# Attention block of a transformer layer: token rows of x permuted over the partitions, and V loaded in three two-row pieces a tile

## Chip, cores and metric

The kernel runs on one core of one Trainium2 chip. The metric is the device time of one execution in microseconds (us), as the median of three runs. An engine name stands for its instruction queue: PE is the matrix engine (TensorE), DVE the vector engine, ACT the scalar engine, POOL GpSimd, and SP the engine that issues nearly all transfers (DMAs).

## The reference, cut to what matters

One transformer layer on 2048 tokens of width 512, in bf16. `mod` gives six vectors from a condition `c`: shift, scale and gate for each of two halves.

```
h = layernorm(x) * (1 + ca) + sa
q, k, v = split(h @ wqkv)                # 32 heads of width 16
logits[s, w] = q[s] . k[s - 2*w] / 4     # w = 0..7; before the first token: -1e9
o[s] = sum over w of softmax(logits)[s, w] * v[s - 2*w]
x = x + ga * (o @ wo)
h = layernorm(x) * (1 + cb) + sb
x = x + gb * ((silu(h @ w1) * (h @ w3)) @ w2)    # inner width 1792
```

Each token looks at itself and at seven earlier tokens, two apart.

## The kernel before, in words

The tokens are cut into 16 tiles T of 128. Token number 128*T + p lies on partition p. A small planner's result is written into the file: `ORDER` is a list of operation numbers, and every engine works through its own operations in the order in which they stand in that list, waiting on semaphores for what they need. `SLOTS` says which buffer each value gets. So an operation that waits holds up everything behind it on its engine, SP's DMA issues among them. A DMA is issued by `Program.dma` (L117, the issue itself is L127).

Stages of the work, with the names that matter below:

- **Loads.** x comes in six DMAs: tiles 0 and 1 alone, 2 and 3 together, then three times four tiles (`x_view`, "(t p) d -> p t d": 128 rows of 1 KB a tile, partition outermost). The modulation weights `wm_s[0]` come in four DMAs (two for the scale, two for the shift, 256 KB each), `wqkv` in six of 256 KB (two each for q, k and v), `wo` in four. The tiny load of `c` (4 rows of 256 bytes) and one of 32 rows of 256 bytes are issued by ACT.
- **First layernorm.** DVE takes statistics of each tile (L579, L580), POOL the power -0.5 (L584, L586), DVE or ACT normalizes. PE turns tiles 0 to 11 with an identity as the moving operand (L663), ACT and DVE evict with the modulation (L672, L673, L680). Tiles 12 to 15 are turned by DMA transposes, and ACT applies the modulation in place (L648).
- **Projections.** k and q (L722, with `wqkv` as the stationary operand; 256 columns a matmul for the first two groups of two tiles, 512 for the others) and v (L749). V is stored to DRAM behind 16 rows of zeros (`v_dram`). Fifteen matmuls on ones (L542) fill the wait for the first data.
- **Attention, by tile.** DVE multiplies q with the eight shifted k's (`prod`, L780, 4096 elements a partition). PE sums over each head's 16 channels with a matrix of ones and zeros `E_sb` (L791, four column groups of 32). Softmax runs on pairs of tiles (L803, L808, ACT's exp L821, L833, L835, L836), and DVE's 32x32 transpose L840 puts the weights beside the V rows. V is loaded again from DRAM, 1 MB a tile in four DMAs of 256 KB: each partition holds two tokens at one of the eight offsets. DVE multiplies in place (`av`, L862, 4096 elements), PE sums over the offsets (L871), ACT evicts (L877), a DMA transposes (`sb_ot`), PE multiplies with `wo` (L895), DVE adds to x (L899).
- **Second layernorm and FFN**, by groups of 2, 2, 4, 4 and 4 tiles: statistics on ACT (L614), POOL (L620, L621), transposes on PE for the first two groups and by DMA for the others, then L911 (w1 and w3), L917, L921, L922, L925, and L953 and L941 with w2. DVE adds x (L969), and one DMA a tile stores 128 rows of 1 KB. Tiles 14 and 15 are stored in two column pieces each.

SP's issues begin with x0, x1, x2-3, the two scale pieces, the two k pieces, the two shift pieces, the two v pieces, x4-7, one q piece, x8-11, the other q piece, x12-15.

Of the kernel before, what the change touches and what calls it, by code (L numbers as in the profile page):

```python
# [21 lines left out]
PAD = 16  # L22
EPS = 1e-5
# [47 lines left out]
def packet_ns(size):  # L71
    return {256: 18, 512: 27, 768: 36, 1024: 48, 2048: 92}[size]


class Program:
# [41 lines left out]
    def dma(self, out, in_, key, packets, r=(), w=(), part=(), after=(), eng="sp", cost=450, group=None, transpose=False,  # L117
            store=False, again=False, pre=()):
        nc = self.nc

        def fn(e):
            a = out() if callable(out) else out
            b = in_() if callable(in_) else in_
            with nc.allow_non_contiguous_dma(reason="layout"):
                for pa, pb in pre:
                    e.dma_start(pa, pb).then_inc(o.inc[0], 16)
                return e.dma_start(a, b, transpose=True) if transpose else e.dma_start(a, b)  # L127
# [3 lines left out]
        ns = 600 if transpose else each * ((PACKET if pre == () and not SHIFTED else 84) if again else packet_ns(size)) + 170 * len(pre)  # L131
        o = self.op(eng, fn, cost, key, r=r, w=w, part=part, after=after, dma=(each, ns, *((900, 200) if store else (1300, 600))))
        o.count = 1 + len(pre)
# [13 lines left out]
    def place(self, order, slots):  # L147
# [10 lines left out]
        for at, o in enumerate(self.placed):  # L158
# [3 lines left out]
            for v in o.vals:  # L162
                if v.pool is not None and v.pool.last.get(v.slot) is not v:
                    before = v.pool.last.get(v.slot)
                    if before is not None:
                        o.prev.extend(before.users)
                    v.pool.last[v.slot] = v

    def synchronize(self):
        known = {e: {} for e in ENGINES}  # L170
        waited = set()
        for o in self.placed:
            e = o.eng
            need = {}
            for d, true in list(o.deps.items()) + [(d, False) for d in o.prev]:
# [77 lines left out]
C_PQ, C_RED, C_ACC, C_TINY = 2203, 440, 864, 90  # L253
# [17 lines left out]
PACKET = 122  # L271
SHIFTED = False
NWARM = 15
DMA_T = (4, 2)
AVCOL = frozenset(range(16))
# [5 lines left out]
def _build(p, A_x, A_wqkv, A_wo, B_w1, B_w3, B_w2, c, w_mod, out):  # L281
# [4 lines left out]
    x_view = x2d.rearrange("(t p) d -> p t d", p=P)  # L286
# [10 lines left out]
    kT = sb([P, KT, PAD + S], bf, "kT")  # L297
# [4 lines left out]
    vshb = [sb([P, 8, D], bf, f"vsh{i}") for i in range(2)]  # L302
# [11 lines left out]
    E_sb = sb([P, KT, H], bf, "E")  # L314
    ones = sb([P, 512], bf, "ones")
    ind = sb([P, 2, 16, 2], bf, "ind")
    before = sb([P, 2, W, 4, 8], bf, "before")
# [26 lines left out]
    zrow = at([PAD, D], bf, "zrow", 25600)  # L344
# [8 lines left out]
    skew = nc.dram_tensor("skew_dram", (NT, 16, 4160), bf) if SHIFTED else None  # L353
# [11 lines left out]
    vshpool = pqpool = Pool("big", pqb + vshb)  # L365
# [8 lines left out]
    def held(pool, items):  # L374

        vals = []
        for i, item in enumerate(items):
# [5 lines left out]
    big_hold = held(vshpool, [vsh_x, vsh_q])  # L383
# [3 lines left out]
    vc, vident, vcst, vE, vind, vbefore = (Val(n) for n in ("const", "ident", "cst", "E", "ind", "before"))  # L387
# [11 lines left out]
    p.op("pool", lambda e: e.memset(E_sb[:], 1.0), 150, k, w=[vE])  # L399
    p.op("pool", lambda e: e.affine_select(out=E_sb[:], in_=E_sb[:], compare_op=ALU.is_ge, fill=0.0, base=0,  # L400
                                           pattern=[[128, KT], [-16, H]], channel_multiplier=1), 320, k, w=[vE])
    p.op("pool", lambda e: e.affine_select(out=E_sb[:], in_=E_sb[:], compare_op=ALU.is_ge, fill=0.0, base=15,
                                           pattern=[[-128, KT], [16, H]], channel_multiplier=-1), 320, k, w=[vE])
    p.op("pool", lambda e: e.memset(ind[:], 0.0), 100, k, w=[vind])
    for r in range(2):
        p.op("pool", lambda e, r=r: e.memset(ind[:, r, :, r], 1.0), 100, k, w=[vind])
    for edge, mult in ((0, 1), (W - 1, -1)):
        p.op("pool", lambda e, edge=edge, mult=mult: e.affine_select(
            out=ind[:], in_=ind[:], compare_op=ALU.is_ge, fill=0.0, base=edge, pattern=[[0, 2], [-W * mult, 16], [0, 2]],
            channel_multiplier=mult), 250, k, w=[vind])  # L410
    p.op("pool", lambda e: e.memset(before[:], 0.0), 250, k, w=[vbefore])
    for q in range(2):
        p.op("pool", lambda e, q=q: e.affine_select(out=before[:, q], in_=before[:, q], compare_op=ALU.is_ge, fill=BEFORE, base=8 * q,
                                                    pattern=[[-DIL, W], [32, 4], [1, 8]], channel_multiplier=0), 400, k, w=[vbefore])
# [695 lines left out]
```

## Time and profile before

| what | value |
|---|---|
| time, median of three runs | 239.54 us (239.43 to 240.87) |
| span of the profiled execution | 237.7 us |
| its own time, if what lies around the span is what median and span leave | 237.7 + 1.8 = 239.5 us |
| busy | PE 229.9, DVE 169.8, ACT 156.4, POOL 23.1 us |
| moved by DMA | 38.3 MB in 44,731 packets |
| granted PE clock | full in every slice |

Busy time is the union of the instructions' spans. A matmul's end is modelled, so a busy PE is not the same as a PE at its peak: whether it is, is read from how many matmuls a stretch holds. The chain that ended last is followed back from the end, from each instruction to what released it. A DMA's share is the mean over the core's 16 DMA engines.

### The profile page before, as it was taken

The numbers are of one execution on the slowest core, as the hardware profiler recorded it, in microseconds if no ns is written. First come the engines' busy times: TensorE is split into PE (matmuls) and PEld (weight loads), VectorE is DVE, ScalarE is ACT, GpSimd is POOL, SyncE is SP. The second block draws the span as 40 slices with busy tenths as digits, with TensorE's granted clock in tenths as the row PEclk, the third lists the DMA queues.
The fourth block names the chain that finished last, engine by engine and source line by source line (L and its number), as shares of the span: only waits on it lengthen the run. The fifth ranks groups of instructions, "written<-read, shape, count | busy, mean of one in ns | idle before, by whom it ended". The sixth has DMA issues, their size and how long they took to land.

```text
span 237.7 us, 4314 instructions
## 1 busy us (share of the span) xinstructions
PE 229.9 (97%) x1665; PEld 120.7 (51%) x1689; DVE 169.8 (71%) x284; ACT 156.4 (66%) x311; POOL 23.1 (10%) x55
## 2 busy tenths in 40 slices
PE   7899998999999999999999999999999999999996
PEld 2667543544568855754434444444344444444454
DVE  4789998999999999999999847379134424042722
ACT  2289798899989987683689799444757926133100
POOL 8323050001001000030000021000001100000000
PEclk9999999999999999999999999999999999999999
DMA  6999999989999977693897484330032142000002
GB/s 185 341 352 351 238 274 179 188 221 297 327 261 273 285 181 223 139 261 69 205 330 116 124 229 105 103 117 0 3 90 88 44 77 80 0 0 0 3 0 88
DMA packets 44731, 38.31 MB, mean 161 GB/s; under 512 B 19736, under 2 KB 36008, under 8 KB 44712
## 3 DMA queue, kind: packets, MB, share of 16 engines
q1 hardware_dynamic: 44656, 38.04, 63.3%
q8 instruction: 13, 0.21, 0.4%
q14 instruction: 6, 0.05, 0.1%
q10 hardware_dynamic: 56, 0.01, 0.0%
HBM read 29.63 MB, written 4.21 MB: 142 GB/s over the span
## 4 chain that ended last, share of the span: by engine, by line
PE 68%; DVE 12%; DMA 7%; ACT 7%; issue 3%; POOL 1%; SPq 1%; DVEq 0%
PE pall L911 38%; PE pall L953 13%; PE pall L722 5%; DMA sb_wo<-in_A_wo_dram 5%; PE pall L895 4%; DVE sb_vsh L862 3%; PE pall L941 3%; DMA sb_wm_s<-in_w_mod_dram 2%; PE pall L871 2%; PE pall L749 2%; ACT sb_h L648 1%; ACT sb_xn L614 1%; PE pall L791 1%; DVE sb_pq L780 1%; DVE sb_pq L862 1%
## 5 line engine op out<-in xcount | busy, mean ns | idle before, releaser
L911 PE MATMUL pall<-sb_h,sb_w 128*128 128x512 bf16 (+1 forms) x554 | 99.6, 336 | 0.5 <-issue 0.2
L911 PEld LDWEIGHTS pall<-sb_h,sb_w 128*128 128x128 bf16 x560 | 52.2, 98 | 47.1 <-ACT sb_sg L917 5.2
L917 ACT ACTIVATE sb_sg<-pall 128x512 bf16<-128x512 f32 (+1 forms) x70 | 33.9, 516 | 29.6 <-PE pall L911 28.6
L953 PE MATMUL pall<-sb_w,sb_hh 128*128 128x512 bf16 x190 | 43.4, 379 | 0.3
L722 PE MATMUL pall<-sb_h,sb_wqkv 128*128 128x512 bf16 (+1 forms) x157 | 30.4, 336 | 1.3 <-ACT sb_v L759 0.8
L953 PEld LDWEIGHTS pall<-sb_w,sb_hh 128*128 128x128 bf16 x196 | 18.9, 98 | 22.7 <-issue 0.4
L921 ACT ACTIVATE sb_hh<-pall 128x256 bf16<-128x256 f32 (+1 forms) x56 | 26.8, 497 | 3.4 <-PE pall L911 3.0
L922 DVE TENSOR_TENSOR sb_hh<-sb_sg,sb_hh 128x256 bf16<-128x256 bf16 (+1 forms) x56 | 17.7, 351 | 12.8 <-ACT sb_hh L921 12.8
L969 DVE TENSOR_TENSOR sb_o<-pall,sb_x 128x512 bf16<-128x512 f32 (+3 forms) x18 | 10.9, 627 | 18.5 <-PE pall L953 13.7
L722 PEld LDWEIGHTS pall<-sb_h,sb_wqkv 128*128 128x128 bf16 x160 | 14.6, 98 | 14.0 <-ACT sb_v L759 1.3
L925 DVE TENSOR_TENSOR sb_hh<-sb_sg,pall 128x512 bf16<-128x512 bf16 x14 | 9.1, 684 | 16.0 <-PE pall L911 15.9
L648 ACT ACTIVATE sb_h<-sb_h,sb_modc 128x512 bf16<-128x512 bf16 x16 | 11.7, 806 | 11.2 <-DMA sb_h<-sb_xn 11.2
L620 POOL TENSOR_SCALAR sb_rs<-sb_var 128x2 f32<-128x2 f32 x8 | 3.4, 427 | 144.4 <-ACT sb_xn L614 144.4
L862 DVE TENSOR_TENSOR sb_pq<-sb_pq,sb_al 128x4096 bf16<-128x4096 bf16 x7 | 15.8, 2285 | 1.0 <-DMA sb_pq<-v_scratch_dram 1.0
L862 DVE TENSOR_TENSOR sb_vsh<-sb_vsh,sb_al 128x4096 bf16<-128x4096 bf16 x7 | 15.9, 2281 | 0.0
L749 PE MATMUL pall<-sb_wqkv,sb_h 128*128 128x512 bf16 x59 | 15.2, 379 | 0.3 <-issue 0.2
L895 PE MATMUL pall<-sb_wo,sb_ot 128*128 128x512 bf16 x60 | 14.9, 379 | 0.6 <-issue 0.5
L673 ACT ACTIVATE sb_h<-pall,sb_modc 128x256 bf16<-128x256 bf16 (+1 forms) x20 | 12.2, 659 | 2.7 <-DVE sb_modc L522 1.8
L780 DVE TENSOR_TENSOR sb_vsh<-sb_q,sb_kT 128x4096 bf16<-128x4096 bf16 x6 | 13.6, 2286 | 0.4 <-ACT sb_q L730 0.4
L625 ACT ACTIVATE sb_xn<-sb_x,sb_nb,sb_rs 128x512 bf16<-128x512 bf16 x16 | 12.4, 818 | 1.9 <-DVE sb_nb L622 1.7
L614 ACT ACTIVATE sb_xn<-sb_x,sb_nm 128x512 bf16<-128x512 bf16 x16 | 11.4, 716 | 2.7 <-DVE sb_nm L610 2.7
L899 DVE SCALAR_TENSOR_TENSOR sb_x<-pall,sb_x 128x512 bf16<-128x512 f32 x16 | 10.7, 678 | 2.9 <-PE pall L895 2.7
(111 smaller groups left out, 254.5 us busy)
## 6 DMA issues: line engine op xcount, KB each, us to landing
sb_pq<-v_scratch_dram SPq DMA_DIRECT2D x28, 256.0 KB, 6.8
sb_vsh<-v_scratch_dram SPq DMA_DIRECT2D x28, 256.0 KB, 5.0
sb_w<-in_B_w_dram SPq DMA_DIRECT2D x6, 512.0 KB, 6.9
sb_w<-in_B_w_dram SPq DMA_DIRECT2D x6, 384.0 KB, 5.9
v_scratch_dram<-sb_v SPq DMA_DIRECT2D x16, 128.0 KB, 5.8
out_dram<-sb_o SPq DMA_DIRECT2D x14, 128.0 KB, 1.8
sb_wqkv<-in_A_wqkv_dram SPq DMA_DIRECT2D x6, 256.0 KB, 6.2
sb_x<-in_A_x_dram SPq DMA_DIRECT2D x3, 512.0 KB, 7.7
```

Source lines behind the costliest of these rows:

```text
L614: p.op("act", lambda e, vn=vn, T=T: e.activation(vn.at[:], x_sb[:, T, :], ACT.Square, bias=nm[:, T, :], scale=D ** -0.5, accum_out=var[:, ...
L648: return e.activation(vh.at[:, ft, 0:n * P], vh.at[:, ft, 0:n * P], ACT.Identity, bias=modc[:, 8 * which + ft:8 * which + ft + 1], scale=m ...
L722: ins = e.matmul(bank(vp)[:, 0:n], wqkv[:, t, kind * D + ft * P:kind * D + (ft + 1) * P], vh.at[:, t, 0:n], start=(t == ORDER[0]), stop=(t ...
L749: ins = e.matmul(bank(vp), vh.at[:, t, tt * P:(tt + 1) * P], wqkv[:, t, 2 * D:3 * D], start=(t == ORDER[0]), stop=(t == ORDER[-1]))
L780: return e.tensor_tensor(bass.AP(vp.at, 0, [[8 * D, P], [KT * P, W], [P, KT], [1, P]]), in0, in1, ALU.mult)
L862: return e.tensor_tensor(v_w, v_w, a_w, ALU.mult)
L895: ins = e.matmul(bank(vy), vt.at[:, ft, :], wo[:, ft, :], start=(ft == 0), stop=(ft == KT - 1))
L911: ins = e.matmul(bank(vp)[:, 0:n], wt[:, t, fi * P:(fi + 1) * P], vh.at[:, t, 0:n], start=(t == 0), stop=(t == KT - 1))
L917: p.op("act", lambda e: e.activation(vt.at[:, 0:n], bank(vgp)[:, 0:n], ACT.Silu), c_act(n), k, r=[vgp], w=[vt], table="silu")
L921: p.op("act", lambda e: e.activation(vh_.at[:, 0:n], bank(vup)[:, 0:n], ACT.Copy), c_act(n), k, r=[vup], w=[vh_])
L922: p.op("dve", lambda e: e.tensor_tensor(vh_.at[:, 0:n], vt.at[:, 0:n], vh_.at[:, 0:n], ALU.mult), 60 + n * 69 // 128, k, r=[vt], w=[vh_], ...
L953: ins = e.matmul(bank(vz), vhh[fi].at[:, tt * P:(tt + 1) * P], w2[:, fi, :], start=(fi == 0), stop=(fi == NF - 1))
```

## The change

Token rows are permuted inside each tile: partition p = 32*j + i now holds token 4*i + j. So x is loaded with a DRAM pattern of [4 rows of step 1][32 rows of step 4][512], one DMA a tile (16 in place of 6), and the result is stored with the same pattern (18 stores, as before). PE's transposes of the first layernorm take an identity whose columns are read in the permuted order, so that h, q, k and v are in token order again; for tiles 12 to 15, turned by DMA, ACT reads in the permuted order from a second buffer. The columns of `wqkv` for q and k are taken with a step of 4, so that partition p of each channel group belongs to head p // 4, and one matrix `ind` serves both sums on PE. The normalization L836 becomes one instruction a tile in place of one a pair.

V: partition 4*i + w' holds tokens 4*i to 4*i + 3 at the two offsets 2*w' and 2*w' + 1, six rows in all, loaded by three DMAs of two rows (256 KB) in place of four. `av` becomes two DVE instructions of 2048 elements with the product in a buffer of its own. The first tile's mask is one matmul in place of two. The code of the `SHIFTED` variant and of `AVCOL`'s other branch, which did not run before either, goes out; `PREL` and `PREA` are empty.

`ORDER` and `SLOTS` are new lists. With the operations counted as the code creates them, SP's new list begins: x0, x1, one scale piece, x2, x3, the other scale piece, the two shift pieces, the two k pieces, x6, a q piece, x8, x7, x4, the other q piece, x5, x10, x14, the 16 zero rows, x15, x9, x13, the two v pieces, x11, a piece of w1, a gate's weights, a piece of wo, the other gate's weights, a piece of wo, x12. On DVE the statistics of tile 11 stand ahead of the first `prod`, and those of tile 12 behind the second. On PE, k and q of tiles 0 to 3 and the transposes of tiles 4 to 7 stand ahead of the first v matmul; from there to the first sum of logits (L791) stand v of tiles 0 to 4, three q or k pieces of tiles 4 to 7, ten transposes and one gate.

```diff
+    def rows(a, T, c0=0, n=D):
+        return bass.AP(a.tensor, a.offset + T * P * D + c0, [[D, TOK], [TOK * D, P // TOK], [1, n]])
+
+    def load_x(T, k):
+        p.dma(x_sb[:, T, :], rows(x2d, T), k, (128, 1024), w=[vx[T]])
...
-        p.dma(x_sb[:, T, :], x_view[:, T, :], ("load", 1), (128, 1024), w=[vx[T]])
+        load_x(T, ("load", 1))
...
-    for g in range(1, 4):
-        p.dma(x_sb[:, 4 * g:4 * g + 4, :], x_view[:, 4 * g:4 * g + 4, :], ("load", 5 + g), (512, 1024), w=vx[4 * g:4 * g + 4])
+    for T in range(4, NT):
+        load_x(T, ("load", 5 + T // 4))
...
+    ident_t = bass.AP(ident, 0, [[P, P], [1, P // TOK], [P // TOK, TOK]])
...
+            vd = vh if which else Val("h", hpool)
...
+                    if not which:
+                        src = bass.AP(vd.at, ft * 512, [[KT * 512, P], [P, n], [1, P // TOK], [P // TOK, TOK]])
...
-                        ins = e.transpose(b[:, col:col + P], vns[tt].at[:, ft * P:(ft + 1) * P], ident[:])
+                        ins = e.transpose(b[:, col:col + P], vns[tt].at[:, ft * P:(ft + 1) * P], ident[:] if which else ident_t)
...
-                    ins = e.matmul(bank(vp)[:, 0:n], wqkv[:, t, kind * D + ft * P:kind * D + (ft + 1) * P], vh.at[:, t, 0:n],
+                    ins = e.matmul(bank(vp)[:, 0:n], wqkv[:, t, kind * D + ft:(kind + 1) * D:KT], vh.at[:, t, 0:n],
...
-                        ins = e.matmul(PALL[32 * q:32 * q + 32, c0:c0 + W * 32], E_sb[:, ft, :], bass.AP(vp.at, ft * P + 8 * q, [[W * KT * P, P], [KT * P, W], [32, 4], [1, 8]]),
+                        ins = e.matmul(PALL[32 * q:32 * q + 32, c0:c0 + W * 32], ind[:],
+                                       bass.AP(vp.at, ft * P + 32 * q, [[W * KT * P, P], [KT * P, W], [1, 32]]),
...
+        for i in range(n):
+            def norm(e, i=i):
...
-        for q in range(4):
...
-                  bass.AP(v_dram, (PAD + T * P + 32 * q) * D, [[2 * D, 16], [-DIL * D, W], [1, 2 * D]]), ("vl", T), (128, 2048),
...
+        for a, n in VLOAD:
+            p.dma(lambda a=a, n=n: vv.at[:, a:a + n, :],
+                  bass.AP(v_dram, (PAD + T * P - DIL * (OFF - 1) + a) * D, [[TOK * D, 32], [-DIL * OFF * D, 4], [1, n * D]]), ("vl", T),
+                  (128, 1024 * n), r=[vv_dram[T]] + ([vv_dram[T - 1]] if T else [vvpad]), part=[vv], group=loads, cost=640)
+        for k in range(OFF):
+            def av(e, k=k):
...
+                return e.tensor_tensor(bass.AP(vp.at, k * TOK * D, [[8 * D, P], [D, TOK], [H, DH], [1, H]]), v_w, a_w, ALU.mult)
...
-        finals.append(p.dma(out2d[T * P:(T + 1) * P, c0:c0 + n], lambda: vo.at[:, 0:n], ("zo", T), (128, 2 * n), r=[vo], cost=400, store=True))
+        finals.append(p.dma(rows(out2d, T, c0, n), lambda: vo.at[:, 0:n], ("zo", T), (128, 2 * n), r=[vo], cost=400, store=True))
```

176 lines of the change are left out of this document (79 added, 97 removed), and 120 rows, old and new, of tables (ORDER, SLOTS).

## The prediction

> **What bounds the kernel now.** First I read the page's shares and the chain that ended last.
>
> ```profile
> span 237.7 us, 4314 instructions
> PE 229.9 (97%) x1665; PEld 120.7 (51%) x1689; DVE 169.8 (71%) x284; ACT 156.4 (66%) x311; POOL 23.1 (10%) x55
> PE 68%; DVE 12%; DMA 7%; ACT 7%; issue 3%; POOL 1%; SPq 1%; DVEq 0%
> ```
>
> PE is busy for all but 7.8 us. Whether it is at its peak shows in two stretches of that chain (start, length, what), one of 256-column matmuls and one of 512-column ones:
>
> ```profile
> 2.69 5.12 DMA sb_wm_s<-in_w_mod_dram
> ...
> 20.68 0.38 PE pall L555 x16
> ...
> 70.11 6.55 PE pall L911 x60
> ...
> 112.24 2.21 DVE sb_vshx L780
> 114.45 0.04 issue
> 114.50 0.62 PE pall L791 x16
> ...
> 146.54 8.91 PE pall L953 x41
> ...
> 235.39 0.02 issue
> 235.41 0.29 DVE sb_o L969
> ```
>
> 6.55/60 = 0.109 us and 8.91/41 = 0.217 us: two halves of one rate, so PE streams without gaps. The first real work waits for a load until 7.81 (2.69 + 5.12); the last matmul ends at 235.39. In between PE has a fixed amount to do in a fixed order, so whatever holds it back for long moves the end by as much. The median is 239.54 us; with 237.7 of span, 1.8 us lie around it, and I take 239.5 as the profiled execution's own time.
>
> What could hold PE back early is the loads. The windows (PE, PEld, DVE, ACT and POOL busy, clock, DMA share, GB/s):
>
> ```profile
> 0.00:6.00 6.00, 4.49 (x11) 1.39 (x11) 2.49 (x7) 1.59 (x2) 4.89 (x22) 1.00 0.64 185
> 6.00:12.00 6.00, 5.25 (x82) 3.84 (x81) 4.42 (x19) 1.39 (x4) 2.16 (x6) 1.00 1.04 342
> 12.00:18.00 6.00, 5.82 (x52) 3.88 (x50) 4.86 (x17) 5.09 (x14) 1.64 (x4) 1.00 1.10 352
> 18.00:24.00 6.00, 5.95 (x65) 4.22 (x64) 5.55 (x19) 6.00 (x15) 1.85 (x5) 1.00 1.08 346
> ```
>
> From 6 us the DMA engines are full at some 350 GB/s, 22 GB/s for each of 16. So the start is paced by the queue of loads, and how a load is shared among the engines matters.
>
> **How many engines a DMA uses.** The packet counts tell:
>
> ```profile
> q1 hardware_dynamic: 44656, 38.04, 63.3%
> ...
> q10 hardware_dynamic: 56, 0.01, 0.0%
> ...
> sb_h<-sb_xn SPq DMA_TRANSPOSE x16, 3.1
> sb_ot<-sb_oa SPq DMA_TRANSPOSE x16, 3.1
> ...
> sb_wm_s<-in_w_mod_dram ACTq DMA_DIRECT2D x1, 8.0 KB, 2.1
> sb_c<-in_c_dram ACTq DMA_DIRECT2D x1, 1.0 KB
> ```
>
> ACT's queue carries 32 + 4 rows but 56 packets. The 20 left are 16 + 4: one closing packet for each engine used, 16 for the load of 16 partitions, 4 for c, whose outermost count is 4. SP's queue fits: counted from the code, 134 plain DMAs carry 25,104 rows (x 2,048; modulation, wqkv, wo and zeros 4,624; w1, w3 and w2 5,888; V stored 2,048 and loaded 8,192; out 2,304); with 134 x 16 = 2,144 closing packets, 17,408 are left for 32 transposes, 544 each = 512 + 2 x 16. Among the 134 are V loads with 16 outermost in DRAM against 128 partitions, and wo's with 32 on both sides; none has an outermost count under 16. The new x loads and stores have 4 outermost in DRAM (`rows`). The trace leaves their number of engines between 4 and 16: c has only four rows, so it could not use more. I take 4, because the one small outermost count in the trace came with that many; 16 is the other end.
>
> The Trainium skill speaks against this change here: "DMA: Bandwidth & Descriptors" (sections "Why a DMA increments its semaphore by 16 and not by 1" and "Rules for kernel authors") says that a DMA runs on the largest number of engines, at most 16, that divides the slowest dimension of both its patterns, so an outermost 4 confines it to four, the lowest-numbered. The counts of c's load agree as far as they go. By it the sum is the one I make.
>
> **The change part by part: x loads.** Terms of before first:
>
> ```profile
> 12.39 1.67 PE L749 MATMUL pall<-sb_wqkv,sb_h 128*128 128x512 bf16 x7
> 27.25 0.29 PE L787 MATMUL pall<-sb_before,sb_ones 128*32 128x256 bf16 x2
> ```
>
> ```profile
> 23.60 6.73 DVE L780 TENSOR_TENSOR sb_vsh<-sb_q,sb_kT 128x4096 bf16<-128x4096 bf16 x3 [0.45 <-ACT sb_q L730]
> 37.64 4.49 DVE L862 TENSOR_TENSOR sb_pq<-sb_pq,sb_al 128x4096 bf16<-128x4096 bf16 x2 [1.01 <-DMA sb_pq<-v_scratch_dram]
> ```
>
> Offset: before, up to wv each engine carries a 16th of x0-3, scale, k, shift and v weights, 5 x 512/16 = 160 KB, 7.4 us at 22 GB/s; V's first matmul runs at 12.39, so data is used some 4.9 us after that count. The scale (64 KB, 3.0 us; landed at 7.81) gives 4.8. I take 4.8.
>
> After, on four engines, an x tile is 32 KB on each instead of 8, and those four are in every other DMA too. Ahead of the first v piece stand 14 x tiles (448 KB) and scale, shift, k, q and half of v (144 KB): 592 KB, 606 thousand bytes. At 22 GB/s they take 27.6 us; the first v matmul could run at 32.4. But 22 is the rate with all sixteen full, and that the total stays at 342 to 352 looks like a common limit; four alone may be faster, at most so much that they carry the whole 350, and then nothing is lost. The forecast takes 25 GB/s, near the row: 24.2 us, first v at 29.0. PE's new order has ahead of it 64 matmuls of 256 columns (7.0 us), 32 transposes of 0.056 (1.8; 128 columns at the same rate) and little else; PE waits, with all later matmuls behind.
>
> From there to the first logits sum: 20 + 12 matmuls of 512 (6.9 us), ten transposes (0.6), one gate (0.4, L555), 7.9 us: 36.9, where the trace has 27.25.
>
> DVE comes out later still: it has tile 11's statistics ahead of its first `prod`, and x11 stands behind v, at 640 KB: 26.2 + 4.8 = 31.0. All of attention is queued behind it on DVE. Then:
>
> ```profile
> L579 DVE BATCH_NORM_STATS2 sb_st<-sb_x 128x6 f32<-128x512 bf16 x16 | 10.3, 675 | 2.8 <-DMA sb_x<-in_A_x_dram 2.8
> L580 DVE BATCH_NORM_AGGREGATE sb_mv<-sb_st 128x2 f32<-128x6 f32 x16 | 2.4, 168 | 0.1
> ```
>
> ```profile
> L584 POOL TENSOR_SCALAR sb_rs<-sb_mv 128x2 f32<-128x2 f32 x7 | 1.5, 218 | 19.0 <-DVE sb_mv L580 17.6 <-DVE sb_modc L522 1.4
> L586 POOL TENSOR_TENSOR sb_rs<-sb_rs,sb_cst 128x2 f32<-128x2 f32 x7 | 6.5, 936 | 0.2
> ```
>
> 0.68 + 0.17 + 0.22 + 2 x 0.94 = 2.9 us: first `prod` at 33.9 instead of 23.60, **10.3 us late**. PE's logits follow DVE, and at 114.50 PE waits for DVE already, so the delay stays to the end. At 22 GB/s it is 37.5, 13.9 late; at the other end 0.
>
> SP issues ten x loads more, behind data that is already late, and sixteen V loads fewer; nothing for either.
>
> **DVE's work.**
>
> ```profile
> L862 DVE TENSOR_TENSOR sb_vsh<-sb_vsh,sb_al 128x4096 bf16<-128x4096 bf16 x7 | 15.9, 2281 | 0.0
> L836 DVE TENSOR_TENSOR sb_attn<-pall,sb_ssum 128x512 bf16<-128x512 f32 x8 | 5.5, 687 | 0.1
> L996 DVE TENSOR_TENSOR sb_w<-sb_w,sb_gb_bc 128x2048 bf16<-128x2048 bf16 x2 | 2.4, 1191 | 0.0
> L969 DVE TENSOR_TENSOR sb_o<-pall,sb_x 128x256 bf16<-128x256 f32 x2 | 0.8, 420 | 1.1 <-PE pall L941 1.1
> ```
>
> `av`: 32 x 1.19 for 16 x 2.28, +1.6 us; normalization: 16 x 0.42 for 8 x 0.69, +1.2. Of these 2.8 us some 1.5 lie ahead of 114.50, where nothing hides them; the 1.0 us that DVE waits for V's DMA at 37.64 is saved by loads a quarter smaller. Net **+0.5** (-1.0 to +1.5). The other 4 MB of V traffic lie behind a busy PE.
>
> **PE and ACT.** Transposes with a permuted identity, 48 of 0.056 us, and q and k weights with a step of 4: no row shows a stepped operand; at no cost 0, at half rate on the transposes 48 x 0.056 = 2.7 us, a third of it in the new wait. A weight load pairs with a matmul in 0.4/16 = 0.03 us (L555) and has 0.109 to hide in. I take 0. The mask matmul is one of two; ACT's permuted reads touch four instructions of the last group.
>
> The Trainium skill's "SBUF — State Buffer", section "Door 1: The DMA port swizzle", asks for two hits in each 16-byte line for full rate. The identity's step of 64 bytes has one, and by it the transposes would cost those 2.7 us; the weights' step of 8 bytes has two. No run here shows either.
>
> **The stores.**
>
> ```profile
> out_dram<-sb_o SPq DMA_DIRECT2D x14, 128.0 KB, 1.8
> ...
> out_dram<-sb_o SPq DMA_DIRECT2D x1, 32.0 KB, 1.4
> ```
>
> Four pieces (128, 96, 64 and 32 KB) follow the last whole tile's w2, within 2 us. On four engines that is 80 KB each, 3.3 us at 25 GB/s, beginning about 0.5 us ahead of PE's end: 2.8 plus some 1 us of landing, where now 2.3 lie between 235.39 and 237.7. **+1.5** (0 to +2).
>
> Sum: 239.5 + 10.3 + 0.5 + 1.5 = 251.8, say **252**; with the row's 22 GB/s 255.4.
>
> **Rivals.**
> - *The x loads run on 16 engines after all.* Then the fetch of x costs what it did, DVE's wait for V goes, and PE's order has nothing to stand on but its own 230 us. For it: no load with few rows outermost and many in all is in the trace. Against: c's count. 239.5 - 1.0 = 238.5: not slower. It decides where an engine's share of an x tile is 8 KB and not 32. 14%.
> - *The same, and the permuted identity halves the transposes' rate:* 238.5 + 2.7 = 241.2. 6%.
> - *Sixteen engines, and the lighter V loads free more than DVE's one wait:* all of PE's idle in mid-run goes, 7.8 less 1.5 and 0.75 in the first two windows and 2.3 at the end = 3.2 us: 236.3. Against: DVE, for which PE waits there, gets 2.8 us more work. 6%.
> - *Four engines, but each well over 25 GB/s* (32: first `prod` at 4.8 + 20.5 + 2.9 = 28.2, 4.6 late): 246. Inside the forecast's case, 16% of all; the forecast proper 52%.
> - *Four engines at less than 22*, as the stores' slope (96 KB more take 0.4 us, 15 GB/s an engine) would have it: first `prod` at 4.8 + 43.7 + 2.9 = 51.4, 27.8 late, 269. 6%.
>
> **How the numbers follow.** The two four-engine cases at 22 to 32 GB/s hold 68%, on 245 to 256.5; that is the likeliest's own range. To leave out only 2 in 10 the range reaches down over the sixteen-engine cases: 238.0 to 256.5. A measurement of this kernel tells about 1%, 2.4 us, from no change. Slower by more: 68 + 6 + 3 (half of the identity's case) = 77%; faster by more: most of the third rival and a tail of the first, 7%; within: 16%.
>
> **What would show it.** Packets on SP's queue: 23,056 rows, 17,408 of transposes, and closing packets of 94 x 16 + 34 x 4 = 1,640 make 42,104; with 16 for each of the 128 plain DMAs it is 42,512. GB/s in the first 24 us falls to about 175 (15 x tiles and 2.6 MB of weights in 26 us) and the DMA share to about half; time to landing of an x tile exceeds 5 us; V's first matmul comes near 29, the first `prod` near 34; the last store lands 3.5 to 4 us after PE's end; PE's busy time is unchanged but for the wait. If the windows still show 340 GB/s, the forecast is wrong at its root; if PE waits for v but the end moves by less than 5 us, the engines were faster.

## The result, and the profile after

| kernel | median | range | ratio to before |
|---|---|---|---|
| before | 240.2 us (4 runs) | 239.43 to 241.06 | |
| changed | 264.02 us (4 runs) | 262.25 to 264.23 | 1.097 (1.092 to 1.102) |

The change costs 24 us, where 12.3 were predicted, and the time lies above the range. One run each of the experiments e5 and e7 further down (250.21 and 248.81 us) fell into a slower state of the chip and is left out there. From the page of the changed kernel, its span, PE's busy time, the granted PE clock in 40 slices of 6.55 us, and SP's queue:

```profile
span 262.1 us, 4352 instructions
...
PE 243.5 (93%) x1688; PEld 129.5 (49%) x1688; DVE 174.3 (66%) x308; ACT 158.7 (61%) x311; POOL 22.0 (8%) x49
...
PEclk9659779999999999999999999999999999999999
...
q1 hardware_dynamic: 42104, 33.84, 45.1%
```

The packets are the 42,104 that four engines for x and out require: the mechanism was there. But PE is busy for 243.5 us and not for 229.9, and its clock is down to 0.5 to 0.7 in four of the first six slices; neither was in the prediction. The stretches of the changed kernel behind the first 6 us (PE, PEld, DVE, ACT and POOL busy, clock, DMA share, GB/s):

```profile
6.00:12.00 6.00, 1.15 (x6) 0.32 (x5) 2.67 (x8) 0.00 (x0) 1.86 (x6) 0.75 0.98 272
12.00:18.00 6.00, 5.99 (x58) 4.07 (x59) 2.54 (x10) 1.40 (x3) 1.61 (x4) 0.50 0.41 133
18.00:24.00 6.00, 6.00 (x63) 5.51 (x61) 4.43 (x14) 4.34 (x12) 1.28 (x4) 0.89 0.28 98
24.00:30.00 6.00, 4.92 (x30) 2.92 (x27) 3.66 (x10) 3.37 (x10) 0.81 (x2) 0.96 0.73 206
30.00:36.00 6.00, 4.96 (x12) 1.62 (x13) 2.33 (x7) 2.35 (x5) 1.40 (x3) 0.50 0.88 245
```

Where before moved 342 to 352 GB/s, it is 98 to 272 here, and between 18 and 24 us a share of 0.28: four engines of sixteen and little more. PE in the same stretch (start, length, line, operation, count, and in brackets its wait and what ended it):

```profile
25.18 3.20 PE L664 MATMUL pall<-sb_ident,sb_xn 128*128 128x128 bf16 x14
...
31.04 7.13 PE L750 MATMUL pall<-sb_wqkv,sb_h 128*128 128x512 bf16 x20 [2.12 <-DMA sb_wqkv<-in_A_wqkv_dram]
...
43.26 0.62 PE L799 MATMUL pall<-sb_pq,sb_ind 128*32 128x256 bf16 x16
```

Three things stand here. V's first matmul waits for v's weights until 31.04 (predicted 29.0). Its 20 matmuls take 7.13 us instead of 20 x 0.217 = 4.3: the clock is 0.50 there. And 14 transposes take 3.20 us, about 0.22 each, where they had 0.056. The window from 24 to 30 us has the clock at 0.96, so that is not the clock. The first logits sum comes at 43.26 instead of 27.25, 16.0 us late; 36.9 was predicted. DVE:

```profile
33.60 0.69 DVE L575 BATCH_NORM_STATS2 sb_st<-sb_x 128x6 f32<-128x512 bf16 x1 [4.31 <-DMA sb_x<-in_A_x_dram]
...
36.24 4.49 DVE L781 TENSOR_TENSOR sb_pq<-sb_q,sb_kT 128x4096 bf16<-128x4096 bf16 x2
```

Tile 11's statistics wait for x as foreseen, and the first `prod` is 12.6 us late instead of 10.3. The groups of the transposes (the kernel before, then the changed one) and of ACT's reads in the changed kernel (busy, mean ns, wait and its end):

```profile
L663 PE MATMUL pall<-sb_ident,sb_xn 128*128 128x128 bf16 x64 | 6.0, 219 | 0.6 <-DVE sb_xn L600 0.6
...
L664 PE MATMUL pall<-sb_ident,sb_xn 128*128 128x128 bf16 x64 | 13.9, 348 | 0.0
...
L650 ACT ACTIVATE sb_h<-sb_h,sb_modc 128x512 bf16<-128x512 bf16 x16 | 13.7, 929 | 9.0 <-DMA sb_h<-sb_xn 9.0
```

Behind the first logits sum PE waits again, at places where it did not before:

```profile
70.03 1.04 PE L750 MATMUL pall<-sb_wqkv,sb_h 128*128 128x512 bf16 x4 [1.22 <-ACT sb_h L650]
...
128.40 0.61 PE L885 MATMUL pall<-sb_vshx,sb_ind 128*32 128x512 bf16 x8 [1.19 <-DVE sb_vshx L872]
134.58 1.04 PE L897 MATMUL pall<-sb_wo,sb_ot 128*128 128x512 bf16 x4 [0.55 <-DMA sb_ot<-sb_oa]
135.85 1.04 PE L897 MATMUL pall<-sb_wo,sb_ot 128*128 128x512 bf16 x4 [0.24 <-DMA sb_ot<-sb_oa]
...
190.73 0.61 PE L885 MATMUL pall<-sb_pq,sb_ind 128*32 128x512 bf16 x8 [1.05 <-DVE sb_pq L872]
...
192.20 0.61 PE L885 MATMUL pall<-sb_pq,sb_ind 128*32 128x512 bf16 x8 [0.42 <-DVE sb_pq L872]
```

The last pieces of PE and DVE work in the changed kernel:

```profile
254.92 2.03 PE L943 MATMUL pall<-sb_w,sb_hh 128*128 128x384 bf16 x22
...
256.99 0.29 DVE L971 TENSOR_TENSOR sb_o<-pall,sb_x 128x128 bf16<-128x128 f32 x1 [0.33 <-PE pall L943]
```

PE ends at 256.95, 21.6 us later than before. From the last DVE instruction to the end of the span it is 262.1 - 256.99 = 5.1 us, before 237.7 - 235.41 = 2.3: +2.8 where +1.5 was predicted. 21.6 + 2.8 = 24.4, the difference of the spans.

### The profile page after: what moved, and what is told of

Same layout as the page of the kernel before. It is cut to its first block, busy times and chain, and to the rows that moved or that the text cites. A ratio compares the mean times of both kernels' runs of the same rounds, so it can differ in the third digit from the quotient of the medians.

```text
span 262.1 us, 4352 instructions
## 1 busy us (share of the span) xinstructions
PE 243.5 (93%) x1688; PEld 129.5 (49%) x1688; DVE 174.3 (66%) x308; ACT 158.7 (61%) x311; POOL 22.0 (8%) x49
## 3 DMA queue, kind: packets, MB, share of 16 engines
q1 hardware_dynamic: 42104, 33.84, 45.1%
## 4 chain that ended last, share of the span: by engine, by line
PE 64%; DMA 12%; ACT 9%; DVE 5%; SPq 5%; issue 2%; POOL 2%; ACTq 0%
PE pall L913 29%; PE pall L955 8%; PE pall L723 8%; PE pall L750 6%; SPq L128 5%; DMA sb_wqkv<-in_A_wqkv_dram 3%; PE pall L664 3%; ACT sb_h L650 3%; DMA sb_x<-in_A_x_dram 3%; PE pall L897 3%; PE pall L885 3%; DMA sb_vsh<-v_scratch_dram 2%; PE pall L943 2%; ACT sb_xn L610 2%; DMA sb_ot<-sb_oa 2%; PE pall L799 2%
## 5 line engine op out<-in xcount | busy, mean ns | idle before, releaser
L913 PE MATMUL pall<-sb_h,sb_w 128*128 128x512 bf16 (+1 forms) x560 | 100.7, 337 | 0.1
L913 PEld LDWEIGHTS pall<-sb_h,sb_w 128*128 128x128 bf16 x560 | 54.2, 98 | 45.3 <-ACT sb_oa L891 1.1
L781 DVE TENSOR_TENSOR sb_pq<-sb_q,sb_kT 128x4096 bf16<-128x4096 bf16 x14 | 31.8, 2279 | 1.3 <-PE pall L799 1.3
L723 PE MATMUL pall<-sb_h,sb_wqkv 128*128 128x512 bf16 (+1 forms) x160 | 32.2, 349 | 0.0
L723 PEld LDWEIGHTS pall<-sb_h,sb_wqkv 128*128 128x128 bf16 x160 | 17.9, 116 | 10.8 <-ACT sb_q L731 0.4
L750 PE MATMUL pall<-sb_wqkv,sb_h 128*128 128x512 bf16 x64 | 18.1, 428 | 3.3 <-DMA sb_wqkv<-in_A_wqkv_dram 2.1
L650 ACT ACTIVATE sb_h<-sb_h,sb_modc 128x512 bf16<-128x512 bf16 x16 | 13.7, 929 | 9.0 <-DMA sb_h<-sb_xn 9.0
L575 DVE BATCH_NORM_STATS2 sb_st<-sb_x 128x6 f32<-128x512 bf16 x16 | 10.8, 685 | 11.3 <-DMA sb_x<-in_A_x_dram 11.3
L872 DVE TENSOR_TENSOR sb_pq<-sb_vsh,sb_al 128x2048 bf16<-128x2048 bf16 x14 | 16.8, 1218 | 2.0 <-DMA sb_vsh<-v_scratch_dram 1.9
L621 ACT ACTIVATE sb_xn<-sb_x,sb_nb,sb_rs 128x512 bf16<-128x512 bf16 x16 | 12.6, 807 | 4.6 <-DVE sb_nb L618 4.6
L664 PE MATMUL pall<-sb_ident,sb_xn 128*128 128x128 bf16 x64 | 13.9, 348 | 0.0
```

The source lines that it names most:

```text
L650: return e.activation(dst, src, ACT.Identity, bias=modc[:, 8 * which + ft:8 * which + ft + 1], scale=modc[:, 8 * which + 4 + ft:8 * which ...
L664: ins = e.transpose(b[:, col:col + P], vns[tt].at[:, ft * P:(ft + 1) * P], ident[:] if which else ident_t)
L723: ins = e.matmul(bank(vp)[:, 0:n], wqkv[:, t, kind * D + ft:(kind + 1) * D:KT], vh.at[:, t, 0:n], start=(t == ORDER[0]), stop=(t == ORDER[ ...
L750: ins = e.matmul(bank(vp), vh.at[:, t, tt * P:(tt + 1) * P], wqkv[:, t, 2 * D:3 * D], start=(t == ORDER[0]), stop=(t == ORDER[-1]))
L781: return e.tensor_tensor(bass.AP(vp.at, 0, [[8 * D, P], [KT * P, W], [P, KT], [1, P]]), in0, in1, ALU.mult)
L872: return e.tensor_tensor(bass.AP(vp.at, k * TOK * D, [[8 * D, P], [D, TOK], [H, DH], [1, H]]), v_w, a_w, ALU.mult)
```

## The experiments

Theory: the x loads and stores on four engines (A), the stepped identity (D), and the clock. Rivals: rows fetched in another order are slow in themselves (C), or the new list of work costs most of it (B). Medians are of four runs (three for e5 and e7, one for e10), the intervals those of the ratio to the kernel before; in all of these runs its median was 239.4 to 240.2.

| run | kernel | median | ratio |
|---|---|---|---|
| e1 | before, x loads by 4 x 32 rows | 257.6 | 1.076 (1.069 to 1.083) |
| e3 | changed, x loads by 16 x 8 rows | 255.2 | 1.065 (1.058 to 1.073) |
| e13 | changed, stores by 16 x 8 rows | 259.6 | 1.077 (1.069 to 1.084) |
| e4 | changed, identity adjacent | 260.8 | 1.088 (1.082 to 1.094) |
| e5 | e3 + e13 + e4 | 245.9 | 1.026 (1.020 to 1.032) |
| e12 | changed, x by 32 x 4 rows in its own layout, identity adjacent | 250.4 | 1.041 (1.035 to 1.048) |
| e9 | e4 + 18 matmuls ahead of v | 260.0 | 1.083 (1.079 to 1.087) |
| e10 | e3 + e13, four steps of the identity (one run) | 246.9 | |
| e7 | e5, ACT's reads contiguous | 244.2 | 1.022 (1.014 to 1.029) |
| e14 | e7, start of the list as before | 246.1 | 1.022 (1.016 to 1.029) |
| e8 | e7, whole DVE products at the later place | 249.1 | 1.039 (1.035 to 1.043) |
| e15 | e7, whole DVE products at the earlier place | 245.6 | 1.024 (1.019 to 1.029) |
| e16 | e7, V fetched from x | 244.5 | 1.019 (1.015 to 1.023) |
| e17 | e7, half of the products left out | 242.9 | 1.013 (1.008 to 1.017) |
| e18 | e16 + e17 | 242.6 | 1.011 (1.008 to 1.014) |

**The x loads alone (e1).**

```diff
+    def rows(T):
+        return bass.AP(x2d.tensor, x2d.offset + T * P * D, [[D, 4], [4 * D, P // 4], [1, D]])
...
-        p.dma(x_sb[:, T, :], x_view[:, T, :], ("load", 1), (128, 1024), w=[vx[T]])
+        p.dma(x_sb[:, T, :], rows(T), ("load", 1), (128, 1024), w=[vx[T]])
```

> The kernel before, with nothing changed but its x loads: each tile is fetched by the change's pattern of 4 x 32 rows. The tokens of a tile are not put back in order, so the output is that of another token order; the work is the same. Theory A (an outermost count of 4 confines a load to four engines, some 22.5 GB/s each): x12 to x15 stand behind 672 KB an engine, landing near 35; with four tiles' statistics and the bias behind it the first prod is at 39 instead of 23.60, and the time is 254 (251 to 258). Rival B (the loads cost little by themselves; most of the 24 us comes from the transposes and the new schedule): below 246. Packets by A: 16 DMAs of 128 + 4 in place of 6 of 1,024 to 128 rows + 16 closing packets.

257.6 us, 18 over before. A wait of PE and the first `prod` of this kernel:

```profile
36.25 0.57 PE L559 MATMUL pall<-sb_csz,sb_wm_g 128*128 128x1 bf16 x16 [4.63 <-DMA sb_wm_g<-in_w_mod_dram]
...
40.83 6.75 DVE L784 TENSOR_TENSOR sb_vsh<-sb_q,sb_kT 128x4096 bf16<-128x4096 bf16 x3 [2.95 <-ACT sb_q L734]
```

40.83, near the 39 of theory A, and 18 us by the x loads alone; B falls. The path differs from A's in its last step: the product no longer waits for x but 2.95 us for q, and PE, which makes q, had stood 4.63 us until 36.25 for a gate's weights. The old list loses more by the four engines than the changed one (18 against the 8.8 us of e3); why, no run separates.

**Sixteen engines for x in the changed kernel (e3).**

```diff
+    def rows16(a, T, c0=0, n=D):
+        return bass.AP(a.tensor, a.offset + T * P * D + c0, [[D, 16], [16 * D, 8], [1, n]])
...
-        p.dma(x_sb[:, T, :], rows(x2d, T), k, (128, 1024), w=[vx[T]])
+        p.dma(x_sb[:, T, :], rows16(x2d, T), k, (128, 1024), w=[vx[T]])
```

> The changed kernel with x loaded by 16 x 8 rows in place of 4 x 32: rows as scattered as before, sixteen as the outermost count, the same number of DMAs. Tokens land on other partitions than the kernel takes them for, so the output is another; the work is the same. Theory A (the outermost count sets the engines): PE's wait for v goes, its 20 v matmuls take 4.3 us and not 7.13, the first logits sum is near 34.5 and not at 43.26, the time 255 (252 to 258). Rival C (the scattered 1 KB rows are slow whichever engines fetch them): 262 or more, first logits sum above 41.

255.2 us, as A has it: rows as scattered, sixteen outermost, 8.8 us back, so C falls. PE of this kernel:

```profile
21.09 3.20 PE L667 MATMUL pall<-sb_ident,sb_xn 128*128 128x128 bf16 x14
...
24.65 6.18 PE L753 MATMUL pall<-sb_wqkv,sb_h 128*128 128x512 bf16 x20
...
35.92 0.62 PE L802 MATMUL pall<-sb_pq,sb_ind 128*32 128x256 bf16 x16
```

V no longer waits, but one point of the expectation failed: its matmuls still take 6.18 us and not 4.3. The clock fell with no wait of PE ahead of it; windows of this kernel (clock in the third column from the right):

```profile
26.00:27.00 1.00, 1.00 (x4) 0.31 (x3) 0.65 (x1) 1.00 (x4) 0.49 (x1) 0.50 0.11 27
27.00:28.00 1.00, 1.00 (x4) 0.31 (x3) 1.00 (x1) 0.66 (x1) 0.00 (x0) 0.50 0.01 2
```

What stands ahead of it are the slow transposes, 14 in 3.20 us. The sum now comes 7.3 us earlier, and still 8.7 later than before.

**The identity (e4), and all three (e5).**

```diff
+    ident_p, vidp = sb([P, P], bf, "ident_p"), Val("ident_p")
+    p.op("dve", lambda e: e.tensor_copy(ident_p[:], bass.AP(ident, 0, [[P, P], [1, P // TOK], [P // TOK, TOK]])), 150, k, r=[vident], w=[vidp])
...
-                        ins = e.transpose(b[:, col:col + P], vns[tt].at[:, ft * P:(ft + 1) * P], ident[:] if which else ident_t)
+                        ins = e.transpose(b[:, col:col + P], vns[tt].at[:, ft * P:(ft + 1) * P], ident[:] if which else ident_p[:])
```

> The changed kernel with the permuted identity copied once into a matrix of its own, by one DVE copy, so that the transposes stream adjacent columns; all else as it is. Theory D (the 64-byte step makes each of the 48 transposes take 0.217 instead of 0.056 us, and those ahead of v are hidden by the wait for v): transposes 3 us of busy time instead of 13.9, the 16 behind v save 2.6 us, time 261 (260 to 262). Rival E (the transposes are slow for another reason, such as the half clock): no change of their mean of 348 ns, 264.

260.8 us, 3.2 back, as theory D has it. The group of the 48 transposes of the first norm in e4:

```profile
L666 PE MATMUL pall<-sb_ident_p,sb_xn 128*128 128x128 bf16 x48 | 5.5, 246 | 0.8 <-DVE sb_xn L598 0.8
```

With the 1.7 us of the other 16 it makes 7.2 instead of 13.9, so the 3 us of the expectation were too low; at 6.0 for 64 in the kernel before they could not be reached. A DVE copy of 0.25 us at the start pays for it. The first logits sum of e4:

```profile
41.79 0.62 PE L801 MATMUL pall<-sb_pq,sb_ind 128*32 128x256 bf16 x16
```

> Three things undone at once in the changed kernel: x by 16 x 8 rows, out stored by 16 x 8 rows, adjacent permuted identity. Tokens land on other partitions, so the output is another; the work is the same. If A and D hold and the stalls of PE in mid-run (66 to 72, 126 to 138, 180 to 200, some 4.7 us) belong to the new V loads and order: 264 - 8.7 - 7.7 - 2.0 = 245.6 (243 to 248). If those stalls are only the late start's: 240 to 241.

245.9 us, as forecast for the case that A and D hold. Alone the three give back 8.8 + 4.4 + 3.2 = 16.4, together some 18; the difference lies within the scatter of the runs. PE of e5:

```profile
18.20 0.97 PE L669 MATMUL pall<-sb_ident_p,sb_xn 128*128 128x128 bf16 x14
...
19.23 4.49 PE L755 MATMUL pall<-sb_wqkv,sb_h 128*128 128x512 bf16 x20
...
27.91 0.62 PE L804 MATMUL pall<-sb_pq,sb_ind 128*32 128x256 bf16 x16
```

The transposes stream at their old rate, v takes 4.49 us, and the first logits sum is at 27.91, where before had 27.25. So all but 0.7 of the 16.0 us at that point are the x loads and the identity. Of the identity alone e4 shows 43.26 - 41.79 = 1.5 us there, of x alone e3 7.3, and the two together 15.4: with late loads the slow transposes are hidden in the wait for v, without them they show: e3, which has the stepped identity, and e5, which differs from it up to there in the identity alone, are 35.92 - 27.91 = 8.0 us apart, with the clock at 0.50 in e3 while v's matmuls run and at 1.00 in e5.

**The same layout on sixteen engines (e12).**

```diff
+        g, q = 4 * (T // 4), T % 4
+        p.dma(x_sb[32 * q:32 * q + 32, g:g + 4, :], bass.AP(x2d.tensor, x2d.offset + (g * P + q) * D, [[TOK * D, 32], [P * D, 4], [1, D]]),
+              k, (128, 1024), part=vx[g:g + 4])
```

> The changed kernel's own layout of x on 16 engines: as many x loads as before (16), but each fetches one block of 32 partitions of four tiles, 32 x 4 rows with 32 as the outermost count, so a tile can be used when its group of four has landed; each group is issued at the place of its first tile. The adjacent permuted identity is in it too; the stores stay on four engines. Theory A (the outermost count sets the engines, whatever the rows): like the kernel with all three parts undone, 246.06, plus 1.9 for the stores and 1.1 for a first tile that waits for 512 KB in place of 128: 249 (247.5 to 250.5), packets on SP's queue 42,104 + 16 x 12 = 42,296. Rival C (this layout is slow to fetch in itself): 258 or more.

250.4 us, within A's range, and the packets expected; C falls here too:

```profile
q1 hardware_dynamic: 42296, 33.84, 50.4%
```

So the layout can be had without the four engines, by loads that take one block of 32 partitions of several tiles. It doesn't win: it stays 4% over before.

**The stores (e13).**

> The changed kernel with only its stores of out by 16 x 8 rows in place of 4 x 32; rows go to other places of out, the work is the same. Theory A for the stores: PE ends as it did, and 3.2 us in place of 5.1 lie behind the last DVE instruction: 264.02 - 1.9 = 262.1 (261.5 to 262.7). Rival: the last store is bound by its own latency, 264.

259.6 us: 4.4 back (3.5 by the spans), not 1.9. The end behaves as expected, 258.6 - 255.46 = 3.1 us behind the last DVE instruction instead of 5.1. The rest is at 190 us, where the changed kernel waits 1.05 + 0.42 us for DVE's product; in this kernel PE runs through:

```profile
189.49 0.61 PE L888 MATMUL pall<-sb_vshq,sb_ind 128*32 128x512 bf16 x8
...
190.79 0.60 PE L888 MATMUL pall<-sb_pq,sb_ind 128*32 128x512 bf16 x8
```

The data traffic between 176 and 196 us in slices of 0.5 us shows why. The changed kernel:

```profile
DMA  0000000058628948932222200000000100560910
GB/s 0 0 0 0 0 0 0 0 115 176 240 104 195 309 105 164 346 98 88 100 94 102 94 29 0 0 0 0 0 0 0 33 0 0 121 142 0 230 32 0
...
sb_vsh<-v_scratch_dram SPq DMA_DIRECT2D x3, 256.0 KB, 4.0
out_dram<-sb_o SPq DMA_DIRECT2D x3, 128.0 KB
...
182.00 6.29 DMA sb_vsh<-v_scratch_dram
```

And e13, between 174 and 194:

```profile
GB/s 0 0 0 0 0 0 0 0 0 0 0 0 0 152 281 303 240 203 272 301 137 242 201 29 0 0 0 0 0 0 0 0 33 0 0 0 23 239 1 128
```

Three V loads and three stores are on their way together. With stores on four engines some 3 us run at 100 GB/s and a share of 0.2, and the last V load, issued at 182.00, takes 6.29 us to land (the last line above, from the chain that ended last); with sixteen, all of it is through in 5.5 us instead of 8. e3, e4, e9 and e12, with stores on four engines, have that wait (1.28 + 0.42 us in e3); e5, e7 and e13 don't.

**The clock (e9).**

```diff
+        if T == 0:
+            def fill(e):
+                for _ in range(18):
+                    ins = e.matmul(bank(vp), ones[:, 0:P], ones[:], start=True, stop=True)
+                return ins
+
+            p.op("pe", fill, 100, k, r=[vc], part=[vp])
```

> The changed kernel with the adjacent permuted identity (260.82), and 18 matmuls of 512 columns of ones put ahead of the first v matmul, in v's own bank, so that PE works through its wait of 3.96 us for v. Theory L (the granted clock falls to 0.50 because PE had nothing to do, and stays there for some 5 us into v's matmuls): the 20 v matmuls take 4.3 us instead of 7.08, the clock is 1.00 from 28 to 36, time 258.1 (257.5 to 258.8). Rival M (the clock falls for another reason): v takes 7 us, time 260.8 or more.

```profile
26.79 3.83 PE L759 MATMUL pall<-sb_ones 128*128 128x512 bf16 x17
31.69 0.60 PE L752 MATMUL pall<-sb_wqkv,sb_h 128*128 128x512 bf16 x2 [1.07 <-DMA sb_wqkv<-in_A_wqkv_dram]
32.61 4.06 PE L752 MATMUL pall<-sb_wqkv,sb_h 128*128 128x512 bf16 x18 [0.32 <-DMA sb_wqkv<-in_A_wqkv_dram]
...
41.41 0.62 PE L808 MATMUL pall<-sb_pq,sb_ind 128*32 128x256 bf16 x16 [1.00 <-DVE sb_pq L790]
...
36.87 4.49 DVE L790 TENSOR_TENSOR sb_pq<-sb_q,sb_kT 128x4096 bf16<-128x4096 bf16 x2
```

Half of theory L holds: with PE at work the clock stays full and v's matmuls take 0.60 + 4.06 us. But the time is 260.0, which neither theory has: 0.8 us back and not 2.7, and that is within the scatter of the runs. V's weights came 0.5 us later in this run, and the first logits sum now waits 1.00 us for DVE, whose products are held by x: it starts at 41.41, when the second product ends (36.87 + 4.49 = 41.36). The half clock ran beside another wait of almost its length.

**The price of the step (e10).**

```diff
+                        st = lambda n: bass.AP(ident, 0, [[P, P], [1, n], [n, P // n]])
```

> One look at the price of the step. The changed kernel with x and out by 16 x 8 rows, and the 64 transposes of the first norm by identities read at steps of 4, 8, 16 and 32 bytes, 16 of each, one line of code each; tokens end up in other places, so the output is another. Theory N (the trace has 0.056 us for adjacent columns and 0.217 for a step of 64 bytes, four times; the price grows with the step until one element a fetch is left): 4 and 8 bytes 0.056, 16 bytes 0.11, 32 bytes 0.217. Rival O (anything not adjacent is four times as slow): all four 0.217. Rival Q, by the Trainium skill's page SBUF — State Buffer, section Door 1: The DMA port swizzle: two hits in each 16-byte line give the full rate, fewer half of it: 4 and 8 bytes 0.056, 16 and 32 bytes 0.11.

In e10 L668 reads at steps of 4 bytes, L669 of 8, L670 of 16 and L671 of 32. From one start to the next, in two places:

```profile
11.21 0.22 PE L668 MATMUL pall<-sb_ident,sb_xn 128*128 128x128 bf16 x1
11.27 0.28 PE L669 MATMUL pall<-sb_ident,sb_xn 128*128 128x128 bf16 x1
...
20.36 0.41 PE L670 MATMUL pall<-sb_ident,sb_xn 128*128 128x128 bf16 x1
20.59 0.41 PE L671 MATMUL pall<-sb_ident,sb_xn 128*128 128x128 bf16 x1
20.82 0.24 PE L668 MATMUL pall<-sb_ident,sb_xn 128*128 128x128 bf16 x1
20.90 0.28 PE L669 MATMUL pall<-sb_ident,sb_xn 128*128 128x128 bf16 x1
21.00 0.29 PE L734 MATMUL pall<-sb_h,sb_wqkv 128*128 128x256 bf16 x1
```

16 bytes take 0.23 us, 32 bytes 0.23 and 8 bytes 0.10, against 0.056 for adjacent columns. 4 bytes take 0.08 behind another stepped transpose, but 0.06 at 11.21, behind a matmul of adjacent columns, and there the transpose is as short (0.22) as one with adjacent columns; so the 0.02 come from what stands ahead, and 4 bytes cost next to nothing. None of the three theories has the whole: 4 bytes are free as N and Q have it, 8 bytes cost some 1.8 times, and 16 bytes already four times. The half rate in Q was the expectation's own estimate, from one hit in place of two.

**ACT's reads (e7), the start (e14).**

```diff
-                        src = bass.AP(vd.at, ft * 512, [[KT * 512, P], [P, n], [1, P // TOK], [P // TOK, TOK]])
+                        src = bass.AP(vd.at, ft * 512, [[KT * 512, P], [1, n * P]])
```

> The kernel with the three parts undone (x and out by 16 x 8 rows, adjacent permuted identity), and now ACT's four permuted reads of the last group made contiguous too. Tokens land on other partitions, so the output is another; the work is the same. That kernel still ran 246.06, 6.7 over the kernel before, and its PE waits 1.21 us for ACT's h at 55.73, behind two pairs of such reads of 2.46 us. Theory G (the step costs ACT 0.5 us each and PE waits for it): each read 0.80 us, that wait under 0.3, time 245.0 (244.3 to 245.7). Rival H (ACT has that much work in this order anyway): the wait moves, time 246.

244.2 us, just under G's range, but the runs reach from 243.7 to 246.3, and the 1.7 us against e5 lie within that scatter. The trace shows what G says. The group in e7, where the changed kernel has 13.7 us and 929 ns:

```profile
L655 ACT ACTIVATE sb_h<-sb_h,sb_modc 128x512 bf16<-128x512 bf16 x16 | 11.9, 814 | 7.9 <-DMA sb_h<-sb_xn 7.9
```

1.8 us less for four reads, and the 1.21 us that PE waits for them in e5 at 55.73 are gone.

> The kernel with x and out by 16 x 8 rows, adjacent identity and plain ACT reads (245.23), and the start of its list put as in the kernel before: the scale's two loads ahead of x2 and x3, and DVE's copy of c ahead of the statistics of tiles 2 and 3. Output as in that kernel. There PE stands idle 1.16 + 0.75 + 0.54 + 0.22 us before 17 us, where the kernel before has 0.56. Theory R (the new order of the start costs that, and all later work follows it): 245.2 - 1.7 = 243.5 (242.8 to 244.3). Rival S (DVE's chain to the first prod sets what follows): 244.6 or more.

246.1 us: theory R falls. PE's waits at the start were a little shorter (1.62 + 0.33 us, where e7 has 1.16 + 0.75 + 0.54 + 0.22), and nothing followed.

**What is left: DVE, and V's way (e8, e15, e16, e17, e18).**

> The one before, and DVE's halves made whole again: one normalization of 512 columns a pair and one product of 4,096 elements a tile, the other half of each replaced by a memset of two columns; the product reads one row of V eight times, and attention's weights are in the order of the kernel before, so the output is another. Theory I (DVE's 2.8 us of halves are what PE waits for, 1.78 us at 45.92 and 1.19 at 113.98): both waits shrink, time 245.0 - 2.5 = 242.5 (241.5 to 243.5). Rival K (DVE waits for V's load, 1.71 us at 40.63, and the halves are covered): PE's wait at 45.92 stays over 1.2, time 244.3 to 245.

249.1 us, slower than with halves: neither theory. The whole product stood where the later of the two halves had stood.

> DVE's halves made whole once more, since e8 put each whole product where the later of its halves stood, and so let PE's input end later. Here the whole stands where the first of the two halves stood and the memset of two columns where the second did; all else as in the kernel with x and out by 16 x 8 rows, adjacent identity and plain ACT reads (245.23). The product reads one row of V eight times and the weights are in the old order, so the output is another. Theory I (what is left over the kernel before comes from the halves and from what the list puts between them: at 111.58 the second half of tile 9 stands behind a bias that waits 0.90 us for POOL, and PE waits 1.18 for it): that wait goes, DVE has 2.8 us less, time 243.7 (242.8 to 244.5). Rival K (the halves are covered): 245 or more.

245.6 us: with the place changed and nothing else the same whole products and normalizations cost 3.5 us less. The halves themselves have no price that can be told here (245.6 against 244.2, with intervals that overlap): K holds.

> The kernel with x and out by 16 x 8 rows, adjacent identity and plain ACT reads (245.23), with V's three loads a tile fetching rows of x in place of the stored V, by the same pattern: they no longer wait for V's stores, which are still made. The output is another. Theory T (what is left over the kernel before is the way of V through DRAM, late for DVE's first products near 40): PE's waits for DVE's product go, time 242 (241 to 243). Rival U (DVE's own work and the order of the list): 244.5 or more.

244.5 us, not told apart from e7's 244.2; T falls.

> The same kernel (245.23) with the second half of every product of attention and V left out, on DVE (a memset of two columns in its place) and in PE's sum (the first half is added twice): half of attention's values are missing, DVE has 16 x 1.15 = 18 us less, PE the same work. Theory V (DVE's amount of work is what PE waits for): PE's waits for DVE's product go, time 242 (241 to 243). Rival: DVE's work is covered and PE waits for V's loads, bias and transposes all the same: 244.5 or more.

> Both at once: V's loads from x without a wait for V's stores, and the second half of the products left out. If V's way and DVE's work together make up what is left: 240 to 241.5, with PE's end within 1 us of the kernel before. If neither does, and it is the order of PE's work itself with the start and the last stores: 243.5 or more.

242.9 us, inside V's range, and 242.6, between the two forecasts for e18. Taking 17 us of work from DVE (173.2 to 156.4 busy) brings 1.3 us by the medians and 1.2 by the spans of e7 and e17 (241.7 and 240.5). The intervals overlap, so the gain isn't clear of noise; the traces show it in one wait, PE's for DVE's product, which is 1.18 us at 112.85 in e7 and 0.30 in e17. V's way brings nothing beside it. In e18 2.6 us over before remain; by the spans it is 2.9, 2.1 of them at PE's end and 0.8 behind it. Its first logits sum, at 29.03, is already 1.8 late; e5 with the same start had 27.91.

## Why the prediction was wrong, step by step

The mechanism behind the forecast, x on four engines, was right, and so was the direction. What failed is the step from late x to a late PE: the lateness that went into the sum was 10.3 us, and the first logits sum came 16.0 late. Terms put small or at nothing failed with it.

- **Four engines for x.** Right: the packets to the last one, in e1, e3 and e12 too. Rate: v's weights at 31.04 give 606 / (31.04 - 4.8) = 23.1 GB/s, tile 11 at 33.60 gives 655 / 28.8 = 22.8. The forecast took 25, above its own row of 22; that is 2.0 us at v and 2.3 at the first `prod`.
- **10.3 for all behind the first `prod`: the step that failed.** The prediction let the lateness of DVE's first product stand for PE's. By DVE alone the first logits sum couldn't have come before 36.24 + 4.49 = 40.73, 13.5 late: it also needs the second product (e9 shows it waiting for that one's end). And it came at 43.26, 2.5 us behind DVE, because PE was later still. The prediction had given PE 7.9 us at full speed from v to this sum; it took 12.2. 2.8 are v's matmuls at half clock, 1.6 the ten transposes at 0.22 instead of 0.056. So 16.0 = 10.3 + 2.34 for the rate + 0.84 for the second product + 2.53 for PE.
- **The permuted identity at 0: a term put at nothing without a row.** "I take 0", with 2.7 as the other end, which assumed half rate at worst. The rate is a quarter, 48 x 0.16 = 7.7 us. Here much of it hides in the wait for x: e4 shows 3.2 of the 24 us; with x on sixteen engines it is 8.0 at the first sum (e3 against e5). The prediction argued from weights, which hide behind the matmuls (in e7, with the step of 4 in q's and k's weights, PE is busy for 230.0 us as before, with 1,662 matmul records against 1,665), while the moving columns have nothing to hide behind. The Trainium skill's "SBUF — State Buffer", section "Door 1: The DMA port swizzle", which the prediction set beside it, speaks of two hits in each 16-byte line for full rate and gives no price for less. By e10 two hits (8 bytes) already cost 1.8 times and one hit four times; the measurement decides.
- **PE's busy time unchanged.** Wrong by 13.6 us by the pages. The page of before lacks 24 of its matmul records, so the better comparison is e5, complete like the changed kernel: 243.5 - 231.8 = 11.7 us, for the transposes and the half clock.
- **ACT's four reads at no cost.** 0.45 us more each, and PE waits 1.22 us for them at 70.03.
- **DVE +0.5.** The direct waits of PE for DVE's product are 1.19 at 128.40, and 1.05 + 0.42 at 190, of which the latter were the stores'. The 4 us by which e7 stays over before were not in the sum; some 0.9 of them hang on the amount of DVE's work (the wait that shrinks in e17), and no experiment isolated the rest. The prediction's range of -1.0 to +1.5 was taken from DVE's instructions, not from where the new list places them: e8 and e15 differ by 3.5 us in that alone.
- **The stores +1.5.** 2.8 at the end, of which e13 takes back 2.0, and 1.5 more at 190 us, where stores and V loads share the four engines. The prediction followed the stores only at the end of the kernel.
- **The sum.** 16.0 at the first logits sum, 1.0 for six more transposes, 4.7 of waits behind it less 1.1 before (0.80 at 40.21 and 0.28 at 114.50), and 2.8 at the end: 23.4 of the 24.4 us by which the spans differ.
- **The rivals.** Sixteen engines (26% of the chances) didn't come true, nor did four engines at 15 or at 32 GB/s. The identity's rival was tied to sixteen engines; it belonged into the four-engine case, and with four times instead of twice the price. The range's upper end, 256.5, summed no second loss on top of 22 GB/s.

What stays open is the last 2.6 to 4 us of the new list, for which no single wait was found. In e18 most of it is there at the first logits sum; what makes that sum late in one run and not in another was not tested.

## What to carry to other kernels

Read a load's outermost count before its bytes: 16 of 128 rows or 32 of 128 keep sixteen engines, 4 make the load as slow as four, and everything that shares those four is slow beside it, stores and loads of the middle of the kernel too. A permutation that costs no instruction isn't free: put it into an operand that is hidden (a weight load) or lay it down once (a DVE copy of 0.25 us), but not into the columns that PE streams, unless the step is 4 bytes. When a loss is hidden by a larger one, undo both before pricing either: x and the identity gave back 7.3 and 1.5 us at the first logits sum alone, and 15.4 together.

## What the runs showed of the hardware

- The moving operand's step: 0.056 us for 128 adjacent columns, 0.06 at 4 bytes (0.08 behind another stepped one), 0.10 at 8, 0.23 at 16 and 32 bytes, and 0.22 at 64.
- PE's clock falls to 0.50 behind a stretch of slow transposes with no wait in it (e3: 14 in 3.20 us, then 0.50 between 26 and 28 us; e5, with the same work at the old rate, keeps 1.00). In the changed kernel, behind a wait, it stays there for some 5 us of full work from 31.04. The Trainium skill's "TensorE: Matmul & The Clock Gate", section "Part 1: The HAM clock gate (the "warmup" mystery)", says that the gate goes by how busy PE was lately and opens after some 3.4 us of work. The trace agrees in kind: e9 fills the wait with matmuls and keeps 1.00, though the 5 us are longer than the 3.4. Why e3's stretch counts little isn't separated: the columns come slowly there, and transposes fill 3.20 us where they fill 0.97 in e5.
- Four engines carry 98 GB/s between 18 and 24 us of the changed kernel, at a share of 0.28, which is 4.5 of sixteen: 22 GB/s each, and 23 by the data that had landed. That is no more than the 22 of each of sixteen at 350.
